# Splitting the block of 128-row matmuls in one step of a chunked attention

## The chip, the cores and the metric

The kernel runs on one core of a Trainium2 chip. The metric is the device time of one execution in microseconds (us). An execution is called slow when it is over 1.5% above the fastest one of the same kernel; in every set of rounds that has any, the slow runs of a kernel have a lower granted TensorE clock than its fast ones. Comparisons of times use fast runs alone. A ratio is the mean time of one kernel's fast runs over that of the other kernel's fast runs of the same rounds on the same chip, so it is not quite the ratio of the medians that are quoted beside it. Brackets after a ratio hold its 95% interval. A step's length and its waits are read from one profiled execution of each kernel.

## The reference, cut to what matters

Two things follow one another: a gated linear attention over 768 tokens (4 sequences, 8 heads of 48), and a balanced mixture of 8 experts over the 3,072 tokens that come out.

```python
def _attn_ref(q, k, v, f_logit):
    f = 1.0 / (1.0 + np.exp(-f_logit))
    for t in range(S):
        state = f[:, :, t, :, None] * state + np.einsum('bhd,bhe->bhde', k[:, :, t], v[:, :, t])
        y[:, :, t] = np.einsum('bhd,bhde->bhe', q[:, :, t], state)
    return y

def _moe_ref(x, w_gate, w1, w2):
    logits = x @ w_gate
    # ... tokens are given to experts in falling order of logits, at most N // E to each
    for e in range(E):
        out[assigned == e] = np.maximum(x[assigned == e] @ w1[e], 0.0) @ w2[e]
```

The change touches the first part alone.

## The kernel before

Attention works on 24 chunks of 128 tokens. Each chunk passes through six stages, and one step of the loop issues one stage of six different chunks, so that all engines have something to do. The order in which a step issues its parts is a list of pairs of a part and a stage; every engine executes its share of that list in that order, and waits by semaphore where data or a buffer isn't ready (in the kernel before, TensorE's x transposes waited three times for x, 1.6 us in all). TensorE's matmuls come in three forms here: on all 128 rows (128*128 in the trace), on half tiles (128*64) and on quarter tiles (48*64). These are the parts that the argument needs, with what they use:

```python
BANKS = {"bank": 6, "sum": 2}                  # PSUM: two rings of banks of 128 x 512 fp32
def ps(name, tag="bank"): ...                  # the next bank of a ring

def decays(G):      # ScalarE: exp of the clamped f, then ln into g
def split(G):       # VectorE: upper <- g;  ScalarE: high <- upper;  GpSimd: low <- g, upper
def sums(G):        # TensorE, 128 rows: L <- high, low (running sums of g)
def factors(G):     # VectorE: dl <- L;  ScalarE: eq, ek <- dl
def clamp(G):       # GpSimd: f <- f, on the loaded input

def transposed(G):  # TensorE, 128 rows: the finished x, turned
    X = spare["X"] = ps("X")
    for d in range(DC):
        nc.tensor.transpose(out=X[:, 128 * d:128 * d + 128],
                            in_=G["x"][:, 128 * d:128 * d + 128], identity=ident[:])
    G["X"] = X

def x_copy(G, work=work):   # VectorE reads columns 0 to D of the same bank
    ...
    nc.vector.tensor_copy(out=G["xT"][:].rearrange("p c t -> p (c t)"), in_=G["X"][:, 0:D])

def halves(G):      # TensorE, half tiles: the "ends" of g, for another chunk
    g = g_bufs[G["i"] % NB]
    bank = spare.pop("X", None)          # spare columns of the X bank of this step
    if bank is None:
        bank = ps("ends")
    G["ends"] = bank[:, D + E:D + E + 2 * HP].rearrange("p (n a) -> p n a", a=HP)
    for hp in range(HP):
        for r in range(2):
            nc.tensor.matmul(out=G["ends"][DP * r:DP * r + DP, :, hp],
                             lhsT=g[:, 2 * hp + r, :], rhs=ind[:], start=True, stop=True)

def gate(G):        # TensorE, half tiles: columns D to D + E of the X bank <- xT, wg
def to_logits(G):   # VectorE: logits <- those columns
def span(G):        # VectorE: spans <- ends;  GpSimd and ScalarE: gl <- spans

def columns(G, nm, t):
    if G["i"] in (1, 2):
        idle_turns(4, ps("nothing", "sum"))   # matmuls whose result nothing reads
    # TensorE, 128 rows: four transposes of qg or kg into T
    ...
def added(G):       # TensorE, half tiles: dS <- v, kg
def new_state(G):   # VectorE: st <- dS, R
def values(G):      # TensorE, half tiles: Y <- v, am
def queries(G):     # TensorE, quarter tiles: Y <- R, qT;  ScalarE: two copies x <- Y
def scores(G):      # TensorE, quarter tiles: A <- qT, kT;  VectorE: am <- mask, A

FIRST = ((decayed, 2), (q_columns, 2), (k_columns, 2), (transposed, 5), (sums, 1))
FILLING = (FIRST + ((x_copy, 5), (factors, 1), (k_copy, 2),
                    (added, 2), (values, 4), (halves, 1), (gate, 5), (gated_q, 1),
                    (new_state, 2), (decays, 0), (gated_k, 1), (span, 1), (to_logits, 5),
                    (split, 0), (clamp, -1), (queries, 4), (scores, 3)))
```

(Bodies are cut to a comment where only the engine and the operands matter; `...` marks other cuts.)

## Time and profile before

| | before |
|---|---|
| median of 3 runs (lowest to highest) | 460.5 us (459.66 to 464.48) |
| profiled span, mean granted clock | 460.6 us, 0.972 |
| start to the x transposes of chunk 0 / chunk 4 / chunk 15 / chunk 23 | 25.7 / 47.4 / 113.8 / 155.2 us |
| an undisturbed step | 5.53 us |
| TensorE, VectorE, ScalarE, GpSimd busy | 95, 57, 30, 29% of the span |

TensorE is the bound, and the attention part is the first third of the time. The busy shares, the slices, a step of the timeline and the fetch holes stand in the prediction.

This is TensorE's timeline of the kernel before, in a step that starts at 80.95 us (start us, duration us, engine, line, operation, output and inputs, tile, shapes, count):

```profile
84.08 0.60 PE L226 MATMUL X<-ind,g 128*64 128x2 f32 x16
```

And this is VectorE's timeline of the kernel before in the same step:

```profile
82.41 0.56 DVE L358 COPY xT<-X 128x384 f32<-128x384 f32 x1
```

VectorE's copy out of bank X ended at 82.41 + 0.56 = 82.97 us, 1.1 us before the ends matmuls wrote into the same bank. Neither line has a bracket, so neither waited.

### The profile page before, as it was taken

What the parts mean: (1) busy time and instruction counts of PE and PEld (TensorE: products, weight loads), DVE (VectorE), ACT (ScalarE), POOL (GpSimd) and SP (SyncE); (2) the same over time, 40 slices, a digit from 0 to 9 for tenths busy, and PEclk for the clock granted to TensorE, in tenths of its full rate; (3) what the DMA queues carried; (4) which work ended last, traced back from release to release, by engine and by line L of the source; (5) the groups of instructions that cost most, each with busy time, mean ns of one, the idle gap of its engine ahead of it and who ended that gap; (6) DMA issues with size and microseconds to landing.
All of it is one profiled execution on the core that took longest, in us unless ns stands there. A gap on an engine that the chain in (4) does not pass through costs nothing. (4 is left out here: it accounts for less than half of the span.)

```text
span 460.6 us, 11925 instructions
## 1 busy us (share of the span) xinstructions
PE 436.4 (95%) x4887; PEld 295.9 (64%) x4887; DVE 261.1 (57%) x878; ACT 139.5 (30%) x322; POOL 133.2 (29%) x189
## 2 busy tenths in 40 slices
PE   8999999899999759999999999999999999999994
PEld 5788989789898535555565565555565555555552
DVE  5788777758688677747637637637637736000000
ACT  4666655546553001212212212212212212212210
POOL 1556655455532012023023023023023026101001
PEclk9999999989999858999999999999999999999999
DMA  9999999978601108082082082072082086500001
GB/s 158 179 199 199 195 188 202 194 156 188 124 27 54 38 19 309 0 291 76 11 292 68 18 292 68 19 290 68 19 290 70 17 286 229 190 18 35 0 19 38
DMA packets 118399, 59.11 MB, mean 128 GB/s; under 512 B 101664, under 2 KB 112960, under 8 KB 118336
## 3 DMA queue, kind: packets, MB, share of 16 engines
q1 hardware_dynamic: 111760, 44.06, 38.4%
q0 software_dynamic: 3072, 9.44, 6.2%
q10 hardware_dynamic: 3504, 4.77, 3.0%
q8 instruction: 40, 0.66, 0.6%
q14 instruction: 23, 0.19, 0.1%
HBM read 48.77 MB, written 9.49 MB: 126 GB/s over the span
## 5 line engine op out<-in xcount | busy, mean ns | idle before, releaser
L1030 PE MATMUL H<-xeT,w 128*128 128x384 f32 x384 | 132.6, 496 | 0.1
L1030 PEld LDWEIGHTS H<-xeT,w 128*128 128x128 f32 x384 | 69.1, 190 | 45.7 <-issue 4.0
L1042 PE MATMUL O<-w,hT 128*128 128x384 f32 x192 | 67.0, 491 | 0.0
L1042 PE MATMUL last_O<-w,hT 128*128 128x384 f32 x192 | 66.7, 491 | 0.0
L1034 ACT ACTIVATE hT<-H 128x384 f32<-128x384 f32 x64 | 31.4, 491 | 101.3 <-PE H L1030 85.3
L1042 PEld LDWEIGHTS last_O<-w,hT 128*128 128x128 f32 x192 | 35.1, 190 | 22.9 <-issue 1.9
L1042 PEld LDWEIGHTS O<-w,hT 128*128 128x128 f32 x192 | 34.9, 190 | 21.5 <-issue 1.3
L1047 POOL DMA_INDIRECT out_dram<-o,token x21 | 21.3, 1014 | 83.6 <-ACT o L1046 83.3
L313 DVE COPY_PREDICATED am<-mask,A 128x512 f32<-128x512 int32 x48 | 32.4, 730 | 17.8 <-PE A L308 17.8
L237 POOL TENSOR_TENSOR kg<-k,ek 128x384 f32<-128x384 f32 x23 | 23.1, 1005 | 48.2 <-ACT ek L215 48.2
L947 POOL TENSOR_TENSOR block<-past 128x72 f32<-128x72 f32 x8 | 2.4, 302 | 111.6 <-DVE at L527 100.1
L308 PE MATMUL A<-qT,kT 48*64 48x128 f32 x768 | 28.6, 284 | 1.9 <-issue 1.2
L1022 ACT COPY xeT<-Xe 128x384 f32<-128x384 f32 x24 | 11.4, 480 | 58.0 <-PE Xe L1019 57.7
L323 PE MATMUL Y<-v,am 128*64 128x48 f32 x768 | 27.0, 223 | 0.3 <-DVE am L313 0.3
L323 PEld LDWEIGHTS Y<-v,am 128*64 128x64 f32 x768 | 24.6, 138 | 1.4 <-DVE am L313 0.8
L989 POOL DMA_INDIRECT xe<-xd,token x21 | 21.5, 1023 | 10.9 <-DVE full L524 4.4
L308 PEld LDWEIGHTS A<-qT,kT 48*64 48x64 f32 x768 | 22.8, 140 | 2.7 <-issue 1.9
L191 POOL TENSOR_TENSOR low<-g,upper 128x384 fp32r<-128x384 f32 x22 | 22.2, 1007 | 7.5 <-DVE upper L188 5.8
L263 ACT COPY qT<-T 128x512 f32<-128x512 f32 x24 | 14.1, 586 | 19.3 <-PE T L255 9.6
L214 ACT ACTIVATE eq<-dl 128x384 f32<-128x384 f32 x24 | 12.6, 524 | 22.8 <-DVE dl L212 22.8
L127 PE MATMUL nothing<-idle,ones 128*128 128x384 bf16 x68 | 17.8, 399 | 1.6 <-DVE ones L132 1.5
L1046 ACT COPY o<-O 128x384 f32<-128x384 f32 x12 | 5.8, 479 | 40.7 <-PE O L1042 40.7
(223 smaller groups left out, 652.8 us busy)
## 6 DMA issues: line engine op xcount, KB each, us to landing
w<-in_moe_w_dram SPq DMA_DIRECT2D x16, 1536.0 KB, 7.3
f<-in_f_logit_dram SPq DMA_DIRECT2D x24, 192.0 KB, 4.7
q<-in_q_dram SPq DMA_DIRECT2D x24, 192.0 KB, 4.8
k<-in_k_dram SPq DMA_DIRECT2D x24, 192.0 KB, 4.7
v<-in_v_dram SPq DMA_DIRECT2D x24, 192.0 KB, 4.8
xd<-x ACTq DMA_DIRECT2D x24, 192.0 KB, 3.1
xe<-xd,token POOLq DMA_INDIRECT x21, 3.1
out_dram<-o,token POOLq DMA_INDIRECT x21, 2.6
```

The lines of the kernel that those rows point to most:

```text
L127: nc.tensor.matmul(out=nothing[:, 0:CAP], lhsT=ones[:], rhs=idle[:], start=True, stop=True)
L191: nc.gpsimd.tensor_tensor(out=low[:], in0=g[:, :, 0:DH], in1=upper[:].bitcast(FP32), op=ALU.subtract)
L237: engine.tensor_tensor(out=G["kg"][:, :, 0:DH], in0=G["k"][:], in1=G["ek"][:], op=ALU.mult)
L263: nc.scalar.copy(out=G["qT"][:].rearrange("p a t -> p (a t)"), in_=G["qTs"][:])
L308: nc.tensor.matmul(out=A[par][HC * j:HC * j + HC, 128 * hp:128 * hp + 128], lhsT=G["kT"][rows, hp, HC * j:HC * j + HC], rhs=G["qT"][rows, ...
L313: nc.vector.copy_predicated(am[:, par], mask[:].unsqueeze(1).to_broadcast((128, HP, 128)), A[par][:].rearrange("s (a t) -> s a t", t=128))
L323: nc.tensor.matmul(out=Y[par][HC * j:HC * j + HC, DH * hp:DH * hp + DH], lhsT=G["am"][:, par, hp, HC * j:HC * j + HC], rhs=G["v"][:, 2 * h ...
L989: nc.gpsimd.indirect_dma_start(out=xe[:], out_offset=None, in_=xd[:, :], in_offset=bass.IndirectOffsetOnAxis(ap=token[:, i:i + 1], axis=0))
L1030: nc.tensor.matmul(out=L["H"][:, 0:CAP], lhsT=L["w1"][:, d, 128 * ft:128 * ft + 128], rhs=xT[:, d, :], start=(d == 0), stop=(d == DC - 1))
L1034: nc.scalar.activation(out=hT[:, ft, :], in_=L["H"][:, 0:CAP], func=AF.Relu)
L1042: nc.tensor.matmul(out=L["O"][:, 0:D], lhsT=hT[:, ft, 128 * i:128 * i + 128], rhs=L["w2"][:, ft, :], start=(ft == 0), stop=(ft == FC - 1))
L1047: nc.gpsimd.indirect_dma_start(out=outs[next(tiles)][:, :], out_offset=bass.IndirectOffsetOnAxis(ap=L["token"][:, i:i + 1], axis=0), in_=o ...
```

## The change

The intent is shorter chains between the engines: x is transposed as soon as it is there, and q and k are transposed just before the quarter tiles that need them. So the block of 128-row matmuls (q, k, x, sums) becomes two blocks: x and sums ahead of the half tiles, q and k ahead of the quarter tiles. On the other engines the parts move as well: decays to the head, split and span earlier. No instruction is added or taken away.

```diff
     def columns(G, nm, t):
-        if G["i"] in (1, 2):
-            idle_turns(4, ps("nothing", "sum"))
...
     def added(G):
+        if G["i"] in (1, 2):
+            idle_turns(8, ps("nothing", "sum"))
...
-    FIRST = ((decayed, 2), (q_columns, 2), (k_columns, 2), (transposed, 5), (sums, 1))
-    FILLING = (FIRST + ((x_copy, 5), (factors, 1), (k_copy, 2),
-                        (added, 2), (values, 4), (halves, 1), (gate, 5), (gated_q, 1),
-                        (new_state, 2), (decays, 0), (gated_k, 1), (span, 1), (to_logits, 5),
-                        (split, 0), (clamp, -1), (queries, 4), (scores, 3)))
-    LAST = ((scores, 3),) + FIRST + ((x_copy, 5), (k_copy, 2), (values, 4), (queries, 4),
-                                     (counts_so_far, 5), (gate, 5), (to_logits, 5))
+    FILLING = ((decayed, 2), (decays, 0), (transposed, 5), (sums, 1), (added, 2), (x_copy, 5),
+               (factors, 1), (split, 0), (halves, 1), (new_state, 2), (values, 4), (span, 1),
+               (gate, 5), (gated_q, 1), (gated_k, 1), (to_logits, 5), (q_columns, 2),
+               (k_columns, 2), (k_copy, 2), (clamp, -1), (queries, 4), (scores, 3))
+    LAST = ((scores, 3), (transposed, 5), (x_copy, 5), (values, 4), (queries, 4),
+            (counts_so_far, 5), (gate, 5), (to_logits, 5))
```

## The prediction

> **What bounds the kernel now.** I read the page's busy shares and 40 slices first, to find the stage that the change touches.
>
> ```profile
> PE 436.4 (95%) x4887; PEld 295.9 (64%) x4887; DVE 261.1 (57%) x878; ACT 139.5 (30%) x322; POOL 133.2 (29%) x189
> PE   8999999899999759999999999999999999999994
> PEclk9999999989999858999999999999999999999999
> DMA  9999999978601108082082082072082086500001
> ```
>
> A slice is 11.5 us. TensorE is near 95% almost everywhere; the input DMA is full for the first eight slices (92 us) and fades in the next three. Attention runs to about 158.8 us (the timeline's first routing counts follow there); the remaining 302 us are routing and expert matmuls, which the diff leaves alone. So only 159 us can move, and 2% of the whole, 9.2 us, would be 5.8% of that stage.
>
> Next I read TensorE's timeline. One undisturbed step of attention, in program order (start us, duration us, what, count):
>
> ```profile
> 101.81 0.66 PE L255 MATMUL T<-ident,qg 128*128 128x128 f32 x4
> 102.31 0.60 PE L255 MATMUL T<-ident,kg 128*128 128x128 f32 x4
> 102.75 0.49 PE L352 MATMUL X<-ident,x 128*128 128x128 f32 x3
> 102.99 0.42 PE L201 MATMUL L<-high,wcum_r 128*128 128x384 f32 x1
> 103.25 0.34 PE L201 MATMUL L<-low,wcum_r 128*128 128x384 f32 x1
> 103.52 0.67 PE L285 MATMUL dS<-v,kg 128*64 128x48 f32 x16
> 104.02 1.10 PE L323 MATMUL Y<-v,am 128*64 128x48 f32 x32
> 104.95 0.60 PE L226 MATMUL X<-ind,g 128*64 128x2 f32 x16
> 105.41 0.50 PE L365 MATMUL X<-wg,xT 128*64 128x8 f32 x12
> 105.84 0.68 PE L337 MATMUL Y<-R,qT 48*64 48x48 f32 x32
> 106.34 1.07 PE L308 MATMUL A<-qT,kT 48*64 48x128 f32 x32
> 107.34 0.66 PE L255 MATMUL T<-ident,qg 128*128 128x128 f32 x4
> ```
>
> The step takes 107.34 - 101.81 = 5.53 us, starts follow without a hole, and the forms change three times: full (128*128), half (128*64), quarter (48*64), full. In the stretch from 101.80 to 107.33, busy times are TensorE 5.53, VectorE 4.38, ScalarE 3.52, GpSimd 3.30 us: TensorE's program bounds the step. But the average is worse. From the q transposes at 46.45 to those at 137.68 fifteen steps take 91.2 us, 6.08 each (though the last two lack dS and are shorter). That is some 8 us of excess, mostly of this kind:
>
> ```profile
> 85.47 0.84 PE L308 MATMUL A<-qT,kT 48*64 48x128 f32 x20
> 87.49 0.65 PE L308 MATMUL A<-qT,kT 48*64 48x128 f32 x12 [1.19 <-issue]
> ...
> 93.53 0.27 PE L337 MATMUL Y<-R,qT 48*64 48x48 f32 x4 [0.82 <-issue]
> ...
> 93.68 1.78 PE L308 MATMUL A<-qT,kT 48*64 48x128 f32 x31
> 95.39 1.11 PE L255 MATMUL T<-ident,qg 128*128 128x128 f32 x4
> ```
>
> "issue" means that no semaphore held it. I counted TensorE records (weight loads, matmuls, waits) up to each hole: 2497, 3777, 4033, 5313 and 5569, all 193 modulo 256. The instruction queue's packets (16 KB each) just before these holes ended only 0.1 to 1.0 us before them. These are late instruction fetches. The five holes are 0.86, 1.46, 1.04, 0.30 and 1.12 us, 4.8 us together. After two of them the granted clock falls to 0.5 for 3.4 us (scores 1.78 instead of 1.07, transposes 1.11 instead of 0.66), about 1.6 us each. So late fetches cost about 4.8 + 3.2 = 8 us.
>
> TensorE's list of waits, and the input f's list:
>
> ```profile
> PE X L352 <- ACT x L344: 1.6, 3, 0.8
>   DMA f<-in_f_logit_dram: 13.1, 6
> ```
>
> The x transposes waited for x three times (25.67, 31.28, 139.57); f's clamp waited for landings in early steps only.
>
> [...] from the last matmul of one form to the first of the next, starts are 0.133 us apart from gate to queries, 0.200 from scores to transposes, 0.268 from sums to dS, 0.203 from x transposes to values; each is the last one's duration less about 0.07. Inside a form they are 0.109 (transposes) or about 0.05 (half tiles) apart. [...] That a burst of loads is what delays a fetch is my inference, not shown. [...]
>
> **The change, part by part.** No instruction is added or removed; the order of the program differs. TensorE's new step is x, sums | dS, ends, values, gate | q and k transposes | queries, scores.
>
> (1) *Form changes.* Four instead of three. Before, scores to q transpose 0.200, k transpose to x transpose 0.109 (same form), gate to queries 0.133: 0.442. After, scores to x 0.200, gate to q transpose 0.203 (gate's duration) - 0.07 = 0.133, k transpose to queries 0.203 as from x to values: 0.536. That is +0.094. A transpose that opens a block is followed 0.164 later by its second, inside the block 0.109; there is one more opening: +0.055. Sum +0.15 us per step, all of it on TensorE's path; over the 20 steps outside the DMA-bound start, +3.0 us.
>
> (2) *Waits between engines.* I laid out one new step from these durations, t = 0 at the x transposes. VectorE: am 0.1 to 1.5, xT to 2.0, dl 2.6, upper 3.0, st 3.3, spans 3.5, qg 4.0, logits 4.2; kT copy from 4.6 (transposes end at about 4.45) to 5.3. Values start at 0.24 + 0.53 + 0.50 + 0.46 = 1.7 and need am at 1.5: just met. x's two copies (0.53) on ScalarE follow the queries; the scores (1.0 us) cover them, with about 0.1 to spare. GpSimd ends kg at about 5.3, dS needs it at 6.5. So I expect no new steady wait, and the late 0.8 us wait for x goes: -0.8.
>
> (3) *Start.* decays is now first on ScalarE, so a late f holds up eq, ek, qT and x as well; before, it came behind qT, eq and ek. f of chunks 4 to 8 is clamped at 22.0, 26.7, 32.0, 36.7, 41.9, straight after landing. From a clamp to the next x transposes ScalarE needs 0.6 + exp and ln 1.03 + eq and ek 1.03 + high 0.5 + qT 0.6 + x 0.53 and latencies: 4.5 us or so. For chunk 7 that gives 41.2, against 41.80 now: near the present pace, not better. The sums of step 3 will wait for high and low near 15.8 with nothing beside them, as the idle matmuls now stand behind the sums (eight at once, same number). I allow +1.0 us, and up to 2 more if the clock halves there.
>
> (4) *Fetches.* Loads go when buffers come free. Now v, q, f and k come free at 3.3, 3.6, 4.4 and 4.5 us into the step beginning at 80.95: a burst. After, f comes free at about 1.1, v 2.7, q 4.0, k 5.3: spread. TensorE also takes 256 instructions in 4.68 us rather than 4.56. Both should make late fetches fewer; I take off half of 8 us: -4.0.
>
> Sum: 3.0 - 0.8 + 1.0 - 4.0 = -0.8. I round to 460.0 us, because the last term is the softest.
>
> **The rivals.** *Form changes alone*: fetches stay as late as they are (their delay was also up to 3.8 us near 121 us, where DMA is less busy, which speaks against bursts) and the start loses 2: 460.5 + 3 + 2 = 465. For it: the parts 1 and 3 are measured or read off an order, part 4 is argued. *Fetches cured*: -8 + 3 - 0.8 + 1 = -4.8, 455.7. For it: loads spread over the step; against: the DMA still has as many bytes, 0.83 busy in the quiet step. *A wait takes over*: x or am late by 0.2 us a step, 24 times, gives 460.5 + 3 + 4.8 + 1 = 469; the margins of 0.1 and 0.2 us above make it possible. *DMA hides all*: in the first 60 us loads come every 4.75 us a chunk, so they don't bind a 5.68 us step for long; this rival would give 458.
>
> **Range and chances.** The known terms span -5 to +5 us around the present time, and the three runs of before spread by 4.8 us. So 455 to 466 holds it 8 times in 10. Over 2% faster (below 451.3) needs more than all fetch losses back: 0.03. Over 2% slower (above 469.7) needs the steady wait: 0.04. Within: 0.93.
>
> **What would show it.** The quiet step 5.68 us from x to x transposes, with four form changes; no waits of x transposes on ScalarE above 0.1 us; fewer or shorter "issue" holes at 193 modulo 256 and fewer half-clock windows before 158 us; x transposes of chunk 4 at 47.4 to 48.5 us; the first routing counts at 158 us give or take 5. I am wrong if a wait on x or am stands in every step, if the start is over 2 us late, if the step is not longer, or if the holes remain.

## More of the kernel before

Keep in mind that one bank X has two users in a step: the transposed x of one chunk, which VectorE copies out as xT, and the ends of another chunk, which land in columns that the copy doesn't read.

The x transposes are the last stage of a chunk, so their starts are good milestones: the stretches between them say where in the pipeline time is lost.

## The result, and the profile after

| | before | after |
|---|---|---|
| median of 4 runs of the same rounds | 461.54 us (459.66 to 464.48) | 479.6 us (476.69 to 483.64) |
| ratio of fast runs | | 1.0391 [1.0291, 1.0492] |
| profiled span, granted clock | 460.6 us, 0.972 | 476.5 us, 0.962 |

The changed kernel is slower by 4%, well outside the predicted range. The page of the kernel after (busy time and share of the span by engine; then tenths of busy time in 40 slices, now of 11.9 us each):

```profile
PE 443.7 (93%) x4887; PEld 298.1 (63%) x4887; DVE 274.7 (58%) x878; ACT 141.7 (30%) x322; POOL 136.2 (29%) x189
PE   8889999999998956999999999999999999999994
PEclk9989999999998965699999999999999999999999
DMA  9999887777710114508127036045054056700001
```

TensorE has the same 4,887 matmuls, busy for 7.3 us more, but the span grew by 15.9. So most of the loss is idle time of TensorE, and the share of busy time falls. The slices are too coarse to show where: attention still reads as nines, because a wait of half a microsecond in every step of six is hidden in them. VectorE is busy for 13.6 us more with the same 878 instructions. One group accounts for it: the 24 multiplies qg take 28.6 us, against 13.6 before (1.24 us each in the quiet steps, against 0.56). The changed order puts qg beside GpSimd's low. VectorE's timeline of the kernel after:

```profile
101.10 1.24 DVE L231 TENSOR_TENSOR qg<-q,eq 128x384 f32<-128x384 f32 x1
```

and GpSimd's timeline of the kernel after:

```profile
100.92 1.01 POOL L191 TENSOR_TENSOR low<-g,upper 128x384 fp32r<-128x384 f32 x1 [2.96 <-DVE upper L188]
```

In all seven profiles of the changed order, in each of the 22 steps in which qg starts beside low, it ends 0.41 to 0.42 us after low ends. It takes 1.24 us where it starts soon after low (after, experiment 4), and 1.09 (experiment 1) or 0.75 (experiment 3) where it starts later: its end follows low's end and not its own start. What the two engines share then, the traces do not show. The longer qg lies off the path here, as VectorE then waits 0.66 us for transposes.

The milestones locate the loss. Each number is a stretch between the starts of x transposes, in us:

| stretch | before | after | difference |
|---|---|---|---|
| start to chunk 0 | 25.7 | 26.6 | +0.9 |
| chunk 0 to 4 | 21.7 | 27.1 | +5.4 |
| chunk 4 to 15 (11 steps) | 66.4 | 69.8 | +3.4 |
| chunk 15 to 23 | 41.4 | 45.4 | +4.0 |
| chunk 23 to the end | 305.5 | 307.6 | +2.1 |

Then one undisturbed step. TensorE's timeline of the kernel after, from x transposes to x transposes, in the columns of before, with idle time and its releaser in a bracket:

```profile
98.14 0.55 PE L352 MATMUL X<-ident,x 128*128 128x128 f32 x3
...
98.96 0.67 PE L285 MATMUL dS<-v,kg 128*64 128x48 f32 x16
100.10 0.63 PE L226 MATMUL X<-ind,g 128*64 128x2 f32 x16 [0.47 <-DVE xT L358]
100.59 1.12 PE L323 MATMUL Y<-v,am 128*64 128x48 f32 x32
101.54 0.49 PE L365 MATMUL X<-wg,xT 128*64 128x8 f32 x12
101.95 0.66 PE L253 MATMUL T<-ident,qg 128*128 128x128 f32 x4
...
102.98 0.68 PE L337 MATMUL Y<-R,qT 48*64 48x48 f32 x32
...
104.48 0.55 PE L352 MATMUL X<-ident,x 128*128 128x128 f32 x3
```

The step takes 104.48 - 98.14 = 6.34 us, against 5.53 before. The third line shown has a bracket: the ends (X<-ind,g) waited for VectorE's xT. They read g, ind and nothing of xT. What they share with xT is bank X, which that copy reads. From dS to ends, starts are 1.14 us apart; from dS to the next part of the same form it was 0.50 before (103.52 to 104.02 in the prediction's lines). So the wait costs 0.64 us; the bracket has 0.47, as it counts from the end of the last matmul before and not from where the next could have started. VectorE's timeline of the kernel after in the same step shows what held the copy:

```profile
98.25 1.35 DVE L313 COPY_PREDICATED am<-mask,A 128x512 f32<-128x512 int32 x2 [0.82 <-PE A L308]
99.50 0.54 DVE L358 COPY xT<-X 128x384 f32<-128x384 f32 x1
```

VectorE cannot start am before it has the scores, the last matmuls of the step before, and am takes until 99.60; behind it comes xT, which ends at 100.04. The ends start at 100.10. Followed from wait to wait this is a closed chain: scores, am, xT, ends, values, gate, transposes, queries, scores. It sets the step. In the list of waits of the kernel after (waiting engine and tile, releaser, us in total, times, longest; first 180 us), it stands 20 times, once for each step in which the ends go to an X bank:

```profile
PEld X L226 <- DVE xT L358: 15.3, 20, 1.9
PE X L226 <- DVE xT L358: 12.4, 20, 1.8
```

The list of the kernel before has no such line. The two lines are the weight loads and the matmuls of the same 20 waits, so they aren't added: 12.4 us of TensorE's idle time.

Now the middle stretch can be summed: 11 steps by (6.34 - 5.53) are 8.9 us of loss, but the difference is only 3.4. Before, the 11 steps took 66.4 - 11 x 5.53 = 5.6 us more than undisturbed ones; after, 69.8 - 11 x 6.34 = 0.1. The holes of "issue" at instruction 193 of 256, five before, are all gone.

### The profile page after: what moved, and what is told of

Read it like the earlier page. It is cut to its first block, busy times and chain, and to the rows that moved or that the text cites.

```text
span 476.5 us, 11863 instructions
## 1 busy us (share of the span) xinstructions
PE 443.7 (93%) x4887; PEld 298.1 (63%) x4887; DVE 274.7 (58%) x878; ACT 141.7 (30%) x322; POOL 136.2 (29%) x189
## 5 line engine op out<-in xcount | busy, mean ns | idle before, releaser
L1042 PEld LDWEIGHTS last_O<-w,hT 128*128 128x128 f32 x192 | 35.2, 191 | 22.8 <-issue 1.9
L231 DVE TENSOR_TENSOR qg<-q,eq 128x384 f32<-128x384 f32 x24 | 28.6, 1191 | 1.7 <-ACT eq L214 1.6
L308 PE MATMUL A<-qT,kT 48*64 48x128 f32 x768 | 26.2, 276 | 0.0
L226 PE MATMUL X<-ind,g 128*64 128x2 f32 x320 | 12.7, 200 | 12.4 <-DVE xT L358 12.4
L308 PEld LDWEIGHTS A<-qT,kT 48*64 48x64 f32 x768 | 21.4, 137 | 0.8 <-issue 0.8
L267 DVE COPY kT<-T 128x512 f32<-128x512 f32 x24 | 16.5, 686 | 8.9 <-PE T L253 8.9
L127 PE MATMUL nothing<-idle,ones 128*128 128x384 bf16 x68 | 19.4, 432 | 1.6 <-DVE ones L132 1.5
```

The costliest lines, as they stand in the source:

```text
L127: nc.tensor.matmul(out=nothing[:, 0:CAP], lhsT=ones[:], rhs=idle[:], start=True, stop=True)
L231: nc.vector.tensor_tensor(out=G["qg"][:, :, 0:DH], in0=G["q"][:], in1=G["eq"][:], op=ALU.mult)
L308: nc.tensor.matmul(out=A[par][HC * j:HC * j + HC, 128 * hp:128 * hp + 128], lhsT=G["kT"][rows, hp, HC * j:HC * j + HC], rhs=G["qT"][rows, ...
L1042: nc.tensor.matmul(out=L["O"][:, 0:D], lhsT=hT[:, ft, 128 * i:128 * i + 128], rhs=L["w2"][:, ft, :], start=(ft == 0), stop=(ft == FC - 1))
```

## The experiments

Theory (S in the expectations): the wait of the ends for xT is most of the loss, and it is there because they share a bank. Rivals: the ends merely inherit time from a chain through am and x that would bind in any case, so that the wait moves elsewhere when it is taken away; the form changes cost more than worked out (F in the expectations); the slower start, from decays at the head of the step, is the larger part. All kernels below gave correct results.

**1. Ends behind values again (in the changed kernel).**

```diff
-               (factors, 1), (split, 0), (halves, 1), (new_state, 2), (values, 4), (span, 1),
+               (factors, 1), (split, 0), (new_state, 2), (values, 4), (halves, 1), (span, 1),
```

> Changed kernel, but with the ends matmuls behind the values matmuls, as in the kernel before. Theory S (the ends write the X bank that VectorE's xT copy still reads, and wait for that copy): the ends no longer stand idle (0.47 us in each step now), the quiet step falls from 6.34 to about 5.68 us, and 20 such steps bring the time from 479.6 to about 466 us. Rival F (the fourth form change is what costs): nothing moves, 479 us. On late fetches: if the slower pace cured them, holes at 193 modulo 256 come back and the time is 468 to 472; if the spread loads cured them, there are none.

Measured: median 476.28 us of 6, ratio to before 1.0326 [1.029, 1.0362]. The step is 6.23 us, far from the 5.68 expected. TensorE's timeline of this kernel says why:

```profile
84.57 0.52 PE L365 MATMUL X<-wg,xT 128*64 128x8 f32 x12 [0.27 <-DVE spans L241]
```

The ends no longer wait. But now the ends stand late, VectorE's copy of them (spans) follows them at once, and the gate, which writes other columns of the same bank, waits for that copy. In the kernel before, spans came behind the gate. The same hazard came back one part later, so this run doesn't tell the theory from the rival of a chain that binds in any case.

**2. A bank of their own for the ends (in the changed kernel).**

```diff
-        bank = spare.pop("X", None)
-        if bank is None:
-            bank = ps("ends")
+        bank = ps("ends")
```

> Changed kernel with its order untouched, but the ends in a bank of their own instead of the X bank. S: the wait of the ends on xT is gone although they stand at the same place, step about 5.68 us, about 466 us, like the run with the ends behind the values; if position rather than the bank mattered, it stays at 479. One more bank is taken in a ring of six each step, so a new wait on a bank is possible, and would show as another releaser. F: 479.

Measured: median 468.57 us of 7, two of them slow. The mean of the five fast runs is 467.7 against 461.7 for before: 1.0138 [1.0104, 1.0172]. In the trace, which fell in a slow run, no ends wait and no other wait takes their place; the undisturbed step is 5.67 us, read before the long half-clock stretch of that run, which begins at 141.9 us. The rival of a chain that binds in any case falls. Some 6 us of loss stay.

**3. The order of before for ends, gate and spans (in the changed kernel).**

```diff
-               (factors, 1), (split, 0), (halves, 1), (new_state, 2), (values, 4), (span, 1),
-               (gate, 5), (gated_q, 1), (gated_k, 1), (to_logits, 5), (q_columns, 2),
+               (factors, 1), (split, 0), (new_state, 2), (values, 4), (halves, 1),
+               (gate, 5), (span, 1), (gated_q, 1), (gated_k, 1), (to_logits, 5), (q_columns, 2),
```

> Changed kernel with the ends behind the values and the copy of the ends (spans) behind the gate, the places they have in the kernel before. The run with the ends behind alone had the gate waiting for the spans copy (0.27 us idle, step 6.23), because gate and ends also share the X bank. S, now worded as 'any order that lets an engine's read of the X bank stand between two TensorE writes to it makes TensorE wait': neither ends nor gate wait, step 5.68 us, time as with the own bank, about 467.5 us. If something else holds the step (qg slowed to 1.24 us beside GpSimd, x just in time), it stays at 6.2 and 476.

Measured: median 472.84 us of 6, three of them slow at clocks of 0.935 to 0.955; the three fast ones average 469.2 against 461.1, which is 1.018. The ratio on record is 1.025 [1.0192, 1.0309], nearer to what all six runs give, and the record doesn't show why; the total of this experiment is therefore not relied on. The trace, a fast one, has neither wait, and the step is 5.79 us instead of the expected 5.68, because the values now come so early that they wait about 0.1 us for am. The bank stays shared, so it is the pair of sharing and order that costs, not the sharing.

**4. Ends in spare columns of the bank of dS (in the changed kernel).** This keeps the changed order and the number of banks in use, and only changes whose bank is shared.

```diff
-        bank = spare.pop("X", None)
+        bank = spare.pop("dS", None)
...
-        G["dS"] = dS = ps("dS")
+        G["dS"] = dS = spare["dS"] = ps("dS")
```

> Changed kernel, order untouched, but the ends are written into the spare columns of the dS bank of the same step (no extra bank), where no engine reads between the dS matmuls and the ends. S: sharing a bank is harmless when no read lies between the writes: no wait of the ends, step 5.67 us as with the own bank, fast runs about 467 to 469 us. If any shared bank makes TensorE wait, the ends still stand idle and it stays near 476 to 480.

Measured: median 468.52 us of 6, one slow; fast mean 468.4 against 462.6: 1.0128 [1.0076, 1.0181]. TensorE's timeline of this kernel:

```profile
88.02 0.55 PE L352 MATMUL X<-ident,x 128*128 128x128 f32 x3
...
88.84 0.67 PE L285 MATMUL dS<-v,kg 128*64 128x48 f32 x16
89.34 0.60 PE L226 MATMUL dS<-ind,g 128*64 128x2 f32 x16
89.80 1.12 PE L323 MATMUL Y<-v,am 128*64 128x48 f32 x32
...
93.69 0.55 PE L352 MATMUL X<-ident,x 128*128 128x128 f32 x3
```

The same ends, in the same place of the order, now start 0.50 us after dS and have no bracket. The step is 93.69 - 88.02 = 5.67 us.

**5. The changed kernel once more, in the rounds of experiment 4.** No edit.

> The changed kernel itself, again, on the chip of the ends-with-dS run, to size the bank wait in the same rounds: 477 to 481 us, step 6.34 us, and a ratio to the kernel before of 1.035 to 1.045. The half-clock window between 140 and 150 us and a longer one after 165 us should be seen again if they belong to the kernel, and not if they were chance.

Measured: median 484.46 us of 6, above what was expected, of which three are slow at clocks of 0.931 to 0.938; the mean of the three fast ones is 479.5 against 462.6: 1.0355 [1.0265, 1.0444]. The step is 6.34 us again, and half-clock windows begin at 140.2 and 174.3 us, as expected. So on one chip and in the same rounds the shared bank costs 479.5 - 468.4 = 11.1 us. An estimate from the trace is 20 x 0.64 = 12.8 us; the intervals of both ratios are wide enough for either number.

**6. The wait put into the kernel before.** If the hazard of bank X is what costs, it must cost there too: spans are copied ahead of the gate, in the order of before.

```diff
-                        (added, 2), (values, 4), (halves, 1), (gate, 5), (gated_q, 1),
-                        (new_state, 2), (decays, 0), (gated_k, 1), (span, 1), (to_logits, 5),
+                        (added, 2), (values, 4), (halves, 1), (span, 1), (gate, 5), (gated_q, 1),
+                        (new_state, 2), (decays, 0), (gated_k, 1), (to_logits, 5),
```

> Reverse test on the kernel before: only the copy of the ends (spans) is moved ahead of the gate, so that VectorE's read of the X bank stands between two TensorE writes to it. S: the gate waits for the spans copy, about 0.4 us idle in each step (ends finish near 105.55 in the quiet step, spans would take until 105.75, the gate began at 105.41), step 5.9 to 6.0 us; 20 such steps are 8 us, of which slower pace may give 2 to 4 us of late fetches back: 465 to 469 us. If sharing the bank is harmless: 461 us.

Measured: median 472.77 us of 4, fast mean 473.4 against 460.2: 1.0279 [1.0218, 1.034]. TensorE's timeline of this kernel has the line of experiment 1 again:

```profile
104.88 0.52 PE L365 MATMUL X<-wg,xT 128*64 128x8 f32 x12 [0.27 <-DVE spans L241]
```

Ends to gate is 0.87 us from start to start (0.45 in the kernel before), and the step is 6.24 us. The loss is larger than I expected: 0.42 us of the 0.71 are this wait, and about 0.3 come from x transposes that then start late. The direction is shown; my size was too small because I had counted the wait and not what it shifts.

**7. The ends moved in the kernel before.** The control for the same item: in the order of before, the ends ahead of the values.

```diff
-                        (added, 2), (values, 4), (halves, 1), (gate, 5), (gated_q, 1),
+                        (added, 2), (halves, 1), (values, 4), (gate, 5), (gated_q, 1),
```

> Kernel before with only the ends moved ahead of the values. S: in the kernel before xT's copy ends at 82.97 and the ends would start at about 83.15, so the same hazard is almost met: at most 0.1 us of wait a step, time 461 to 464 us. If the place of the ends alone cost time, it would be some 13 us slower, 475.

Measured: 461.16 us of 20, ratio 1.000 [0.9977, 1.0023], step 5.53. In this order the ends would take the place that the values had, 83.15 us in the step shown of before, and xT was copied at 82.97: ready with 0.2 us to spare. The reason is that the transposes of q and k still lie between the scores and those of x (0.94 us from q to x in the prediction's lines, 101.81 to 102.75), so that VectorE has done with am when x is transposed. Moving the ends ahead of the values is harmless by itself; it costs in the new order, in which the x transposes open the step. Experiment 3 is the other half of this: the new order with the ends behind the values (and spans behind the gate) has no such wait either. The cause is a pair of moves, and no one line of the diff shows it.

**8. The transposes of q and k moved, with what that needs (in the kernel before).**

```diff
+    FILLING = ((decayed, 2), (transposed, 5), (sums, 1), (x_copy, 5), (factors, 1),
+               (added, 2), (values, 4), (halves, 1), (gate, 5), (gated_q, 1),
+               (new_state, 2), (decays, 0), (gated_k, 1), (span, 1), (to_logits, 5),
+               (split, 0), (clamp, -1), (q_columns, 2), (k_columns, 2), (k_copy, 2),
+               (queries, 4), (scores, 3))
```

> The kernel before in all but one thing: the q and k transposes and the kT copy stand ahead of the queries (with the idle matmuls placed as in the changed kernel, which this needs). Four form changes instead of three, ends behind values, decays late. S: quiet step 5.68 us, 0.15 above 5.53, so about 461.5 + 3 = 464.5 us, with late fetches as before. F: most of the 18 us shows here, 475 us or more.

(The idle matmuls and LAST, the order of the last steps, are those of the changed kernel.) Measured: 471.52 us of 6, ratio 1.02 [1.0163, 1.0237]. It was meant to price the form changes, and it doesn't, for a new wait is in the list of waits of this kernel:

```profile
PE X L352 <- ACT x L344: 7.0, 12, 1.4
```

With decays still late in ScalarE's order, the copies of x come too late for transposes at the head of the step; steps are 5.78 to 6.3 us. What it does show: with decays late, x transposes at the head wait. A first build of this kernel, with the idle matmuls left in the q and k columns, deadlocked: they take a bank of the ring "sum" between values and queries, while both of its banks are held. So the change had to move the idle matmuls too.

**9. Decays at the head alone (in the kernel before).**

```diff
-    FILLING = (FIRST + ((x_copy, 5), (factors, 1), (k_copy, 2),
+    FILLING = (FIRST[:1] + ((decays, 0),) + FIRST[1:] + ((x_copy, 5), (factors, 1), (k_copy, 2),
...
-                        (new_state, 2), (decays, 0), (gated_k, 1), (span, 1), (to_logits, 5),
+                        (new_state, 2), (gated_k, 1), (span, 1), (to_logits, 5),
```

> The kernel before with only decays moved to the front of the step, as in the changed kernel, so that f's buffer comes free early and loads are less bunched. If spread loads cure late fetches: fewer and shorter holes at 193 modulo 256, up to 8 us less in the steps after 47 us, at a start that may be 1 to 3 us later: 455 to 460 us. If only pace matters: step 5.53 us, holes as before, 461 to 464 us.

Measured: 464.78 us of 8, fast mean 464.6 against 461.7: 1.0067 [1.0033, 1.0102]. The x transposes of chunk 4 come at 51.9 us instead of 47.4, 4.5 us later; some of it is regained in the profiled run and 2.9 us stay in the mean. This is GpSimd's timeline of this kernel at the start:

```profile
20.76 0.99 POOL L237 TENSOR_TENSOR kg<-k,ek 128x384 f32<-128x384 f32 x1 [2.50 <-ACT ek L215]
...
22.23 1.01 POOL L191 TENSOR_TENSOR low<-g,upper 128x384 fp32r<-128x384 f32 x1
23.21 0.51 POOL L172 TENSOR_SCALAR f<-f 128x384 f32<-128x384 f32 x1
```

and this is ScalarE's timeline of this kernel just behind it:

```profile
23.75 0.52 ACT L177 ACTIVATE f<-f 128x384 f32<-128x384 f32 x1 [1.09 <-POOL f L172]
```

GpSimd waits for ek, then does kg, low and last the clamp of the next f; ScalarE waits for that clamp with its first instruction of the step, and eq and ek come behind it. So each engine waits for the other: a ring. In the next three steps low also waits 0.5 to 0.8 us for upper, which VectorE does behind qg and so behind eq: the ring goes through VectorE too. The clamps of f of chunks 4 to 8 come at 23.2, 29.1, 35.2, 40.8 and 46.4 us, 5.8 apart on average; before they stood at 22.0, 26.7, 32.0, 36.7 and 41.9, 5.0 apart, the first two of them behind a wait for the landing. In this kernel none of these five waits for a landing: their f had landed 2.4 to 6.4 us before. So the ring, not the landing of f, sets the pace of this start, and the 4.5 us by which the last of these clamps is late match the 4.5 us of chunk 4. The changed kernel has the same wait in its list:

```profile
ACT f L177 <- POOL f L172: 15.0, 8, 3.1
```

But there 10.5 of the 15.0 us belong to the first four chunks, whose clamps did wait for landings; 4.5 us are left for the ring.

**10. The idle matmuls back at the head of the sums (in experiment 2's kernel).** A rival for the slow start is that the idle matmuls stand too late.

```diff
     def sums(G):
+        if G["i"] in (2, 3):
+            idle_turns(8, ps("nothing", "sum"))
...
     def added(G):
-        if G["i"] in (1, 2):
-            idle_turns(8, ps("nothing", "sum"))
```

> The own-bank run with one more edit: the eight idle matmuls of steps 3 and 4 stand ahead of the sums instead of behind them, so that they fill the 2 us in which TensorE waits for high. Theory: the idle TensorE at 13 to 15 us lets the clock halve in the start (windows at 15 to 31 us in all runs with the idle matmuls behind the sums, none in the kernel before): no such window, 1 to 3 us faster than the own bank's 467.6, about 465.5. Rival: the start is held by f's landings alone: same 467.6, x of chunk 4 still near 51.6 us.

Measured: 470.02 us of 6, ratio 1.0173 [1.0132, 1.0215]. The x transposes of chunk 4 start at 51.4 us, against 51.6 in experiment 2. The half-clock window that the move was to remove came all the same (3.4 us, at 18.2 us; in experiment 2 at 15.6). So this move doesn't help the start, and that idle time of TensorE is what halves the clock stays a theory, not shown here.

**11. Decays at the head from step 9 on (in the kernel before).** Experiment 9 took 63.9 us from chunk 4 to 15 against 66.4 before. If that gain is real, it should stay when the start is spared.

```diff
+    EARLY = FIRST[:1] + ((decays, 0),) + tuple(p for p in FILLING[1:] if p[0] is not decays)
...
-            for part, stage in FILLING if step < len(chunks) + 2 else LAST:
+            for part, stage in (FILLING if step < 9 else EARLY) if step < len(chunks) + 2 else LAST:
```

> Kernel before, with decays first only from step 9 on, when loads are no longer just in time. Theory: decays first costs 4 us at the start (x of chunk 4 at 51.9 instead of 47.4 us in the run with decays first) and gives back about 2.5 us from step 9 on through fewer late fetches: here only the gain is left, 458 to 460 us against 461.9. Rival: the gain was luck of one profile: 461 to 463 us.

Measured: 460.73 us of 14, ratio 0.9999 [0.9976, 1.0022]. Chunk 4 is back at 47.1 us, which confirms that early decays cost time only at the start. The middle takes 65.9 us with four late fetches; there is no gain to keep.

**12. One more buffer for each input (in the kernel before).** The late fetches vanish in the changed order. If bursts of loads delay them, buffers that come free a step earlier might ease it.

```diff
-                          bufs={"f": 3, "q": 4, "k": 4, "v": 7}[nm])
+                          bufs={"f": 4, "q": 5, "k": 5, "v": 8}[nm])
```

> Kernel before with one more buffer each for f, q, k and v (4, 5, 5, 8), so that no load waits for the release that makes the four of a step leave together; they then go as earlier loads land. If bunched loads make the late fetches: fewer holes at 193 modulo 256, up to 5 us faster, 456 to 459 us, and a version better than both. If the total of bytes on the queues is what delays them (loads would now run at full rate until about 115 us): holes as before or worse, 461 to 465 us.

Measured: 460.76 us of 14, ratio 1.0012 [0.9983, 1.004], with three late fetches (0.65, 0.9 and 1.3 us). The same. (The 115 us of the expectation is an estimate: 24 chunks at the prediction's 4.75 us each are 114.) No version was found that beats the kernel before.

The late fetches across all these kernels, counted in one profile of each, in the stretch from 22 to 150 us, as holes of 0.28 us or more at 193 modulo 256:

| kernel | order | step, us | holes |
|---|---|---|---|
| before; experiments 7, 9, 11, 12 | before | 5.5 | 5; 5, 4, 4, 3 |
| experiment 6 | before, with a wait | 6.24 | 4 |
| experiment 8 | before, q and k moved | 5.8 to 6.3 | 4 |
| experiments 2, 4, 10 | changed, without the bank's wait | 5.67 | 2, 1, 0 |
| experiment 3 | changed | 5.79 | 0 |
| experiment 1; after, twice | changed | 6.2 to 6.3 | 0; 0, 0 |

A slower pace is not the cure: experiment 6 has 6.24 us and four holes, experiment 10 has 5.67 us and none. The changed order is the cure. Loads are spread in it: after the x transposes their median issue is at 1.3, 3.6, 4.2 and 5.3 us (f, v, q, k), against 2.4, 2.9, 3.6 and 4.6 (v, q, f, k) before. That fits, but experiments 9 and 11 move f alone and experiment 12 gives more buffers, and none of them cured it. Which part of the order does it stays open.

## Why the prediction was wrong

**The form changes were right.** The prediction's part (1) has +0.15 us per step. Experiments 2 and 4 show 5.67 against 5.53: +0.14, so 2.8 us over 20 steps against 3.0. The parts agree too: from scores to x, gate to q and k to queries, starts in experiment 4 are 0.200, 0.134 and 0.202 us apart, against 0.200, 0.133 and 0.203 in the prediction.

**The failed step is in part (2):** "Values start at 0.24 + 0.53 + 0.50 + 0.46 = 1.7 and need am at 1.5: just met", and from it "So I expect no new steady wait". The layout asked of each TensorE part whether its inputs were ready. It put the ends at 0.24 + 0.53 + 0.50 = 1.27 us, and on the line for VectorE it had "xT to 2.0", both nearly right (measured: 1.32 without the wait, and 1.90). It never set these two numbers beside each other, because the ends don't read xT. They write into the bank that xT's copy reads. The layout by itself gives 2.0 - 1.27 = 0.73 us of wait per step, 20 steps, so 14.6 us; the trace has 0.64, and 11.1 us are what the runs of experiments 4 and 5 show. The rival "A wait takes over" was the right kind at 0.04, with the wrong waits (x or am), and at 4.8 us less than half of the size.

In the traces the wait goes by the bank, not by the address: the ends wait for a copy of other columns of the same bank (0.64 us), so does the gate (0.27 us idle in experiments 1 and 6), and with another bank the ends don't wait (experiments 2 and 4). What the hardware would do without this wait no run here shows.

**The x margin held.** The prediction allowed 0.1 us for x's copies. Scores to x transposes are 0.200 us from start to start, as expected, and no real wait for x stands in the quiet steps.

**The start was mis-sized, for a reason that was not the one given.** Part (3) has +1.0 us at the start, from f landing late for ScalarE. Decays at the head alone move chunk 4 by 4.5 us, and the total by 2.9 (experiment 9). What binds there is the ring of clamp, exp, ek, kg and low. The prediction's chain from clamp to x transposes took the clamp as "straight after landing"; it left out that GpSimd gives the clamp the last place, behind kg and low, and that these now wait for what ScalarE does after the clamp. In the changed order low comes first and waits for VectorE's upper (12.0 us in four waits from 26 to 54 us), so the ring is a similar one and not the same; no run tests it by itself there. Experiment 3's kernel has the changed order without the bank's wait and without a half-clock window before chunk 4; its chunk 4 is at 51.4 us, 4.0 late. In the changed kernel chunk 4 is at 53.7 us, 6.4 late and outside the 47.4 to 48.5 that the prediction named. The ends' waits (3.4 of their 12.4 us lie before chunk 4) and a half-clock window of 3.4 us at 30.8 (about 1.6, by the prediction's own count) add to the 4.0 only in part, as the three would make 9.0. Two small slips of the prediction change nothing: f of chunks 7 and 8 was clamped 0.8 us after it landed, not straight after, and 460.5 + 3 + 2 is 465.5, not 465.

**The late fetches went, as part (4) said, and more fully.** It took off 4.0 us; in the middle stretch 5.6 us of excess became 0.1. The reason given (bursts of loads) is not shown.

**A loss after chunk 15 was not foreseen.** In the profile after, chunks 15 to 23 take 4.0 us more. Five of the ends' waits lie there, with 3.9 us of TensorE's idle time (they are up to 1.1 us long, as the last three come in steps without dS, which put the ends still earlier). But kernels without the bank's wait also lose in this stretch: +1.8 us in experiment 4, +5.7 in experiment 10. A half-clock window begins at 140 to 148 us in all profiles of the changed order (experiments 1 to 5 and 10) and in none of the order of before. What starts it was not settled. The last stretch differs by 2.1 us, but in profiles of the order of before it varies from 305.5 to 308.1, so I read nothing from it.

The account then is: form changes 2.8, the bank's wait 11.1, decays at the head 2.9 (from 4.5 at chunk 4), in sum 16.8. The means of the fast runs differ by 479.5 - 462.6 = 16.9 us in experiment 5, and by 479.9 - 461.8 = 18.1 in the first rounds. That agreement is partly luck: the terms come from different chips and rounds, and two are not in the sum, the fetches gained (5.5 us in the middle stretch) and the late stretch (+1.8 in experiment 4). Without the bank's wait the rest does not close. Experiment 4's profile is 6.6 us longer than that of before: 6.6 us later at chunk 4, 3.4 us gained from there to chunk 15, 1.8 and 1.6 us lost in the last two stretches. So its start costs more than 2.9 or 4.0 us. A half-clock window of 10.2 us, from 14.4 us on, lies in that start; experiment 1 has one of 13.7 us, experiment 3 none. What starts them stays open.

## What to carry to other kernels

When an order changes, list for every buffer, and for every PSUM bank as a whole, who reads and who writes it in a step, and lay out write after read as well as read after write: parts that shared nothing but a bank waited for each other here (0.64 us a step). Check pairs of moves, since two moves that are harmless alone can meet in one bank. In a pipeline of several engines, also look for rings, in which the last instruction of one engine feeds the first of another.

## Prices that these runs show

- One more change of form per step cost 0.14 us here (5.67 in experiments 2 and 4 against 5.53).
- The holes taken for late fetches lie at 193 modulo 256 and last 0.28 to 1.98 us, and whether they came at all depended on the order of the program (3 to 5, or 0 to 2).
- In the kernel before, the clock fell to half after holes of 1.46 and 1.04 us (at 86.0 and 92.5, window at 93.9) and after one of 1.12 us (at 123.2, window at 124.6), with TensorE busy in between. Both half-clock stretches lasted 3.4 us. What makes the clock fall is not shown.
- The wait for the shared bank cost 11.1 us of 479.5 here, in 20 waits (experiments 4 and 5).
